# Attention with two feed-forward layers: words converted later, parked sums copied and stored by ScalarE

## The chip, the cores and the metric

One NeuronCore of one Trainium2 chip runs the whole kernel. The metric is the device time of one execution in microseconds (us), taken as the median of several runs. TensorE (PE) multiplies matrices and writes its results to PSUM banks, VectorE (DVE) and ScalarE (ACT) do elementwise work, GpSimd (POOL) does a little, and SyncE (SP) issues DMAs. Each engine takes its own instructions strictly in order and waits where a result of another engine is missing.

## The reference

Three layers follow each other. Attention: 4 batches, 8 heads, head size 64, 512 local tokens and 32 global ones. Global queries see all 544 keys; a local query sees the 32 global keys and the local keys at most 32 positions away. The result has 2176 rows of 512 numbers.

```python
s_ll = np.where(np.abs(pos[:, None] - pos[None, :]) <= 32, scale * q_l @ k_l.T, -1e9)
a_l = softmax(concat([scale * q_l @ k_g.T, s_ll]))     # local rows; global rows see k_all
x = a @ concat([v_g, v_l])                             # (2176, 512) over batches and heads
h = x @ w_in1;  x = (max(h, 0) ** 2) @ w_out1          # d_ff = 2048
h = x @ w_in2
P = a0 + a1*h + a2*h**2 + a3*h**3
Q = 1 + |b0|*|h| + |b1|*h**2
out = (P / (Q + 1e-6)) @ w_out2
```

The four weight matrices arrive as 64-bit floats; all else is 32-bit.

## The kernel before, in words

**Weights.** Each layer's hidden dimension is cut into 16 slices f of 128. A slice has two halves, a piece of `w_in` (half 0) and one of `w_out` (half 1). A half arrives as 64-bit words and has to be made into 32-bit floats by integer work; then it is split into a high and a low part, so that three fast matmuls give a 32-bit product. Here one half is called a *word item*. Its steps, with their engines: load into a tile `S` (SP, `w_load`, L125); `abs` (ACT, L142), which takes a fresh tile `T`; `elow` (POOL, L150); `clamp`, `shift`, `sign`, `add` (DVE, L145, L156, L160, L165); then `hi` and `lo`. For the first five slices `hi` is an ACT copy into the weight tile (L178) and `lo` a DVE subtraction (L185). For slices 5 to 10 of the first layer, `hi` is an SP store of the finished `T` to a scratch tensor in HBM (L170) and `lo` does nothing; the item is read back later.

**Ticks.** `cv_tick` is the clock of these steps. At each tick every item under way grows one tick older and does the steps whose age is listed in its table; every `per` ticks a new item is loaded. The item keeps the table that `cv["at"]` held when it was loaded. `OX` has `abs` at age 8, `clamp` at 9, `add` at 10, `hi` at 13, `lo` at 14. There are three `S` tiles and four `T` tiles.

**The attention stage.** 41 steps i = 0 to 40, five to a unit (half a batch's heads). Each step issues the scores of one group, softmax work of others, transposes (`T`, `tr`), the product with the values (`PV`) of group i, and four ticks at its end. Vectors of `v` are loaded into window tiles (`vw`, `big`) and then copied inside SBUF by four DMAs (L608 to L611).

**Fill jobs.** From step F0 = 11 on, TensorE also does part of the first feed-forward layer in each attention step: `f_h` (`H`, L511, 12 matmuls) for job i-11 and `f_y` (`Y`, L541, 12 matmuls) for the job before it. Jobs run over tokens in segments of 256 with slices 0 to 4. At the last job of a segment the two banks `Y` hold a sum that is *parked*: copied to two tiles `pk` (L551) and stored to the HBM tensor `park` (L552); the two segments that add to an earlier sum load it first (L518) and add on DVE (L548). The `pk` tiles come out of the same four as `T`. Sums without an addition are parked at steps 13, 15, 26, 31, 36 and after step 40, called parks 1 to 6; those with an addition at steps 18 and 21. In steps from 11 on, `tr`, `T`, `PV` and `H` have one PSUM bank each, so the next user of a bank waits until ACT or DVE has read it.

**DMA counters.** Every DMA raises one of eight completion counters, used in turn. A DMA waits for the one that used its counter before it. In the listings below `DMAHW5_49` is counter 5; `PE_49`, `DVE_49`, `Activation_49`, `Pool_49` are the counters of the engines.

**After the attention** the rest of both layers runs, 699 us, with TensorE the busy engine.

Of the kernel before, what the change touches and what calls it, by code (L numbers as in the profile page):

```python
# [23 lines left out]
def kernel(  # L24
# [36 lines left out]
    pe, ve, sc, gp, sy = nc.tensor, nc.vector, nc.scalar, nc.gpsimd, nc.sync  # L61
# [4 lines left out]
    def bank(tag):  # L66
        i = turns[tag].pop(0)
        turns[tag].append(i)
        return ps.tile([128, 512], F32, tag=f"b{i}", name=tag)
# [123 lines left out]
    todo, line, cv = [], [], dict(z=4, at=None, per=8, lo=ve)  # L193
# [22 lines left out]


    OX = dict(abs=8, elow=8, clamp=9, shift=9, sign=9, add=10, hi=13, lo=14)
    OE = dict(abs=4, elow=4, clamp=5, shift=5, sign=5, add=6, hi=9, lo=10)
    OL = dict(abs=2, low=3, clamp=3, shift=4, sign=4, add=5, hi=7, lo=9)  # L220
    OS = dict(hi=5, lo=8)
    ORD = ("hi", "add", "lo", "clamp", "shift", "sign", "low", "elow", "abs")
# [259 lines left out]
    def fill(i):  # L482
        return fp.tile([128, (10, 4, 2)[i] * NSUB], F32, tag=f"f{i}", name=f"f{i}")

    frows, fturn, fx, fh, fg, fy, fpk = [], dict(x=0, h=0), {}, {}, {}, [], []
# [16 lines left out]
    def f_park(a, i):  # L502
        return park[:, 2 * i:2 * i + 2, NSUB * a:NSUB * a + NSUB]

    def f_h(q):
        seg, a, f, _, last, add = fjobs[q]
        while (0, f, 1) not in done:
            cv_tick(LEFT[1])
        w, h = wt[0, f], bank("H")[:, 0:NSUB]
        for m, (k, s, t) in enumerate([(k, s, t) for k in range(NK) for s, t in ((0, 0), (1, 0), (0, 1))]):  # L510
            pe.matmul(h, w[:, s, 0, 128 * k:128 * k + 128], fx[seg, k][t], start=m == 0, stop=m == 3 * NK - 1)  # L511
        if last:
            for k in range(NK):
                fx.pop((seg, k))
            if add:
                for i in range(2):
                    t = cv3.tile([128, 512], U32, tag="T", name="pk").bitcast(F32)
                    sy.dma_start(t.rearrange("p (m t) -> p m t", m=2), f_park(a, i))  # L518
                    fpk.append(t)
        i = fturn["h"] = (fturn["h"] + 1) % 2  # L520
        hi, lo = [frow(1, 2 * i + z).bitcast(F32R) for z in range(2)]
        g = frow(2, i)
        sc.activation(g, h, AF.Relu)
        sc.activation(hi, g, AF.Square)
        fh[q], fg[q] = (hi, lo), (g, h)
# [6 lines left out]
    def f_y(q):  # L532
        _, a, f, first, last, add = fjobs[q]
        hi, lo = fh.pop(q)
        w = wt[0, f]
        if first:
            fy[:] = [bank("Y"), bank("Y")]
        ms = range(NK)
        for m, z in [(m, z) for m in ms for z in range(2)] + [(m, 2) for m in ms]:

            pe.matmul(fy[m // 2][:, NSUB * (m % 2):NSUB * (m % 2) + NSUB], w[:, z % 2, 1, 128 * m:128 * m + 128],  # L541
                      (hi, hi, lo)[z], start=first and z == 0 and m % 2 == 0, stop=last and z == 2,
                      skip_group_check=True)
        if last:
            for i in range(2):
                if add:
                    t = fpk.pop(0)
                    ve.tensor_tensor(out=t, in0=fy[i], in1=t, op=ALU.add)  # L548
                else:
                    t = cv3.tile([128, 512], U32, tag="T", name="pk").bitcast(F32)  # L550
                    (sc.copy if i else ve.tensor_copy)(t, fy[i])  # L551
                sy.dma_start(f_park(a, i), t.rearrange("p (m t) -> p m t", m=2))  # L552


    with ExitStack() as at:
# [14 lines left out]
        def load_qk(n, i):  # L570

            b, hq = divmod(n, 2)
            src, dst, nm = ((q_l, qraw, "qr"), (k_l, kraw, "kr"))[i]
            t = raw1 if n == 1 and not i else raw.tile([128, 4, 4, D], F32, tag=nm, name=nm, bufs=1 + i)
            x = src[b, 4 * hq:4 * hq + 4].rearrange("h (p c) d -> c p h d", c=4)
            for c in range(4):
                sy.dma_start(t[:, c], x[c])
            dst[n] = t
# [10 lines left out]
        def load_v(n, part):  # L589
            b, hq = divmod(n, 2)  # L590
            hs = slice(4 * hq, 4 * hq + 4)
            w = vw[n % 2]
            wf = w.rearrange("p w h d -> p w (h d)")
            A, Bw, C = wf[:, 0:5], wf[:, 5:10], wf[:, 10:14]
            vg = v_g[b, hs].rearrange("h g d -> g h d")
            vl = v_l[b, hs]
            if part == 0:
                for a in range(5):
                    sy.dma_start(w[0:96, a, :, 0:D], vl[:, 96 * a:96 * a + 96].rearrange("h p d -> p h d"))
                sy.dma_start(w[96:128, 9, :, 0:D], vl[:, 480:512].rearrange("h p d -> p h d"))  # L600
                for p, a in ((96, 0), (64, 5), (32, 10)):
                    sy.dma_start(w[p:p + 32, a, :, 0:D], vg)
                return
            if part == 2:
                for p, t, m in ((96, A, 4), (64, Bw, 4), (32, C, 3)):
                    gp.tensor_copy(t[p:p + 32, 1:], t[p:p + 32, 0:1].to_broadcast([32, m, 4 * (D + 1)]))
                return
            sy.dma_start(Bw[0:64], A[32:96])  # L608
            sy.dma_start(Bw[96:128, 0:4], A[0:32, 1:5])
            sy.dma_start(C[0:32], A[64:96, 0:4])  # L610
            sy.dma_start(C[64:128], A[0:64, 1:5])  # L611
# [13 lines left out]
        for i, pair in enumerate(some):  # L625
            for h in range(4):
                p, m = slice(32 * h, 32 * h + 32), pair[h % 2]
# [91 lines left out]
        F0 = 11  # L719
# [165 lines left out]
        for i in range(NS + 1):  # L885
            (n, g), pos, fq = groups[min(i, NS - 1)], i % 5, i - F0
            if i == F0 - 1:
                turns.update(T=[2], PV=[3], tr=[4])
                frows.extend(fill(z) for z in range(3))
            for c in (LD0 if n == 0 else LD)[pos] if i < NS else ():  # L890
                if c in "qk":
                    m = n + 2 + (c == "k" and pos == 4)
                    if m < 2 * B:
                        load_qk(m, "qk".index(c))
                elif n + 1 < 2 * B:
                    load_v(n + 1, "ABR".index(c))
            if i + 2 < NS:
                pend.pop(i + 2)()
            late = i + 2 < NS and groups[i + 2][1] == 4
            quo = list(st_r.pop(i - 1)) if i else []  # L900
            low = []
            if i + 3 < NS and not late:
                low, pend[i + 3] = do_S(i + 3)
            for op in itertools.chain(*itertools.zip_longest(quo, low)):
                if op:
                    op()
            for dn, z in PZ0[pos] if n == 0 else PZ[pos]:
                if i < NS and n + dn < 2 * B:
                    prep(n + dn, z)

            if 0 <= fq < len(fjobs):
                f_h(fq)
            if i + 1 < NS:
                do_T(i + 1)
            if 0 <= fq < len(fjobs):
                f_low(fq)
            if i >= 2:
                do_xT(i - 2)
            if i + 3 < NS and late:
                low, pend[i + 3] = do_S(i + 3)  # L920
                for op in low:
                    op()
            if 0 < fq <= len(fjobs):
                f_y(fq - 1)
            if i < NS:
                do_PV(i)
            if fq == -1:
                for k in range(NK):
                    f_split(0, k)
            elif 0 <= fq:  # L930
                for d, ks in ((1, range(1, NK)), (2, range(1))):
                    if fq + d < len(fjobs) and fjobs[fq + d][3]:
                        for k in ks:
                            f_split(fq + d, k)
            if i == 0:
                prep_g(0)
            if i == 1:
                sy.dma_start(coef[:, 0:4], a2.rearrange("(o a) -> o a", o=1).to_broadcast([128, 4]))
                sy.dma_start(coef[:, 4:6], b2.rearrange("(o a) -> o a", o=1).to_broadcast([128, 2]))
            if i == 10:  # L940
                sc.activation(coef[:, 6:8], coef[:, 4:6], AF.Abs)
            if i == F0 - 3:
                cv.update(z=0, per=4)
            if i == F0:
                cv["at"] = OE
            if i == F0 + 3:
                cv["per"] = 7
            for _ in range(4):
                cv_tick(LEFT[1])
        do_xT(NS - 1)  # L950
# [44 lines left out]
```

## Time and profile before

| what | value |
|---|---|
| median of 3 runs | 948.52 us (947.42 to 950.25) |
| the profiled execution | 951.82 us, span of its instructions 950.0 us |
| TensorE busy | 906.0 us, 95% of the span |
| VectorE busy | 731.0 us, 77% |
| ScalarE busy | 619.6 us, 65% |
| attention stage | ends at about 251 us of the span |

The page gives, for one execution, the busy time of each engine, a strip of 40 slices of the span, DMA queues, the chain of work that ended last, and the costliest groups of instructions. Other views list the instructions of one engine in order of time (with the idle time before each and what ended it), sum waits by who waited for whom, or give busy time and granted TensorE clock by stretch. TensorE's busy time is near the span, but not evenly: the strip shows where it was not.

### The profile page before, as it was taken

To read this page: it belongs to the slowest core of one execution; us is meant where nothing else is said; L and a number is where in the kernel's file an instruction comes from. 1 tells how busy PE (TensorE), PEld (TensorE's weight loads), DVE (VectorE), ACT (ScalarE), POOL (GpSimd) and SP (SyncE) were. 2 spreads that over 40 slices of the span, in tenths; PEclk is the share of its full clock that TensorE was granted. 3 is DMA by queue.
4 is the path that set the end of the run, shared out by engine and by line. 5 is a ranking of instruction groups with operands and counts; after the bars stand their busy time and mean duration, and the time that the engine had idled before them with its cause. 6 is when DMAs were issued, how large, how long until landed. Compare 5 with 4: busy or idle time off the path is not lost.

```text
span 950.0 us, 19472 instructions
## 1 busy us (share of the span) xinstructions
PE 906.0 (95%) x7440; PEld 824.9 (87%) x7440; DVE 731.0 (77%) x1743; ACT 619.6 (65%) x1331; POOL 56.0 (6%) x109
## 2 busy tenths in 40 slices
PE   7886898998999999999999999999999999999997
PEld 4665787887899999999999998989989989989875
DVE  3687886778468577576766469999989989989896
ACT  3675664565478555454544457787787787787886
POOL 5223122120000000000000000000000000000000
PEclk9898799999999999999999999999999999999999
DMA  9997687662265264455422340010010010010000
GB/s 191 181 197 153 143 234 197 169 158 91 79 172 152 78 185 143 140 186 164 161 89 78 133 177 0 1 34 1 1 34 1 1 34 1 1 34 1 19 16 22
DMA packets 106477, 91.55 MB, mean 96 GB/s; under 512 B 60304, under 2 KB 89488, under 8 KB 106384
## 3 DMA queue, kind: packets, MB, share of 16 engines
q1 hardware_dynamic: 106384, 90.31, 35.6%
q8 instruction: 58, 0.95, 0.4%
q14 instruction: 35, 0.29, 0.1%
HBM read 63.18 MB, written 20.19 MB: 88 GB/s over the span
## 4 chain that ended last, share of the span: by engine, by line
PE 76%; DVE 7%; DMA 6%; ACT 6%; issue 2%; SPq 1%; ACTq 0%; DVEq 0%
PE S L306 31%; PE y L386 18%; PE y L383 13%; PE H L511 3%; DMA S<-in_moe_w_out_dram 3%; PE Y L541 3%; DMA S<-in_moe_w_in_dram 2%; PE tr L707 1%; PE S L740 1%; PE PV L834 1%; PE PV L839 1%; DVE T L160 1%; PE T L794 1%; DVE T L165 1%; DMA vw<-vw 1%
## 5 line engine op out<-in xcount | busy, mean ns | idle before, releaser
L306 PE MATMUL S<-big,w 128*128 128x384 f32 (+1 forms) x1776 | 330.7, 327 | 2.0 <-ACT big L288 1.1
L306 PEld LDWEIGHTS S<-big,w 128*128 128x128 f32 x1776 | 298.2, 188 | 9.1 <-DVE ts L346 2.1
L386 PE MATMUL y<-w,big 128*128 128x512 f32 x816 | 209.1, 398 | 4.2 <-ACT big L364 2.9
L386 PEld LDWEIGHTS y<-w,big 128*128 128x128 f32 x816 | 149.4, 188 | 38.2 <-DVE big L365 7.9
L383 PE MATMUL y<-big,w 128*128 128x384 f32 (+1 forms) x912 | 161.0, 326 | 1.7 <-DVE big L332 0.9
L383 PEld LDWEIGHTS y<-big,w 128*128 128x128 f32 x912 | 150.8, 188 | 2.4 <-DVE big L332 1.2
L342 ACT ACTIVATE big<-S 128x384 f32<-128x384 f32 (+1 forms) x96 | 45.6, 475 | 75.9 <-PE S L306 72.6
L321 ACT ACTIVATE big<-S 128x384 f32<-128x384 f32 (+1 forms) x76 | 35.6, 468 | 85.2 <-PE S L306 83.6
L329 DVE TENSOR_TENSOR big<-big 128x384 f32<-128x384 f32 (+1 forms) x60 | 31.3, 522 | 74.1 <-ACT big L325 73.9
L345 DVE TENSOR_TENSOR ts<-ts,S 128x384 f32<-128x384 f32 (+1 forms) x96 | 50.8, 529 | 24.8 <-ACT ts L343 24.5
L306 PE MATMUL S<-xm,w 128*128 128x384 f32 (+1 forms) x288 | 67.8, 327 | 0.0
L344 ACT ACTIVATE tq<-big,coef 128x384 f32<-128x384 f32 (+1 forms) x96 | 66.1, 689 | 0.0
L142 ACT ACTIVATE T<-S 128x512 f32<-128x512 f32 x64 | 42.9, 670 | 34.2 <-DMA S<-in_moe_w_in_dram 13.4
L343 ACT ACTIVATE ts<-S,coef 128x384 f32<-128x384 f32 (+1 forms) x96 | 62.5, 651 | 0.0
L346 DVE SCALAR_TENSOR_TENSOR ts<-ts,coef,S 128x384 f32<-128x384 f32 (+1 forms) x96 | 56.9, 592 | 3.4
L325 ACT ACTIVATE big<-big 128x384 fp32r<-128x384 f32 (+1 forms) x76 | 38.2, 503 | 30.2 <-PE y L383 29.7
L306 PEld LDWEIGHTS S<-xm,w 128*128 128x128 f32 x288 | 52.2, 188 | 2.9
L358 DVE SCALAR_TENSOR_TENSOR ts<-tq,ts 128x384 f32<-128x384 f32 (+1 forms) x96 | 51.4, 536 | 3.3
L541 PE MATMUL Y<-f,w 128*128 128x256 f32 x360 | 52.1, 295 | 1.2 <-ACT pk L551 1.2
L511 PE MATMUL H<-f,w 128*128 128x256 f32 x360 | 52.3, 296 | 0.0
L365 DVE TENSOR_TENSOR big<-ts,big 128x384 fp32r<-128x384 f32 (+1 forms) x96 | 50.7, 528 | 0.2 <-ACT big L364 0.2
L347 DVE TENSOR_TENSOR tq<-tq,big 128x384 f32<-128x384 f32 (+1 forms) x96 | 50.7, 529 | 0.0
(132 smaller groups left out, 1314.9 us busy)
## 6 DMA issues: line engine op xcount, KB each, us to landing
S<-in_moe_w_out_dram SPq DMA_DIRECT2D x32, 512.0 KB, 4.3
S<-in_moe_w_in_dram SPq DMA_DIRECT2D x32, 256.0 KB, 5.6
S<-in_moe_w_in_dram SPq DMA_DIRECT2D x16, 512.0 KB, 4.6
scr<-T SPq DMA_DIRECT2D x24, 256.0 KB, 2.5
T<-scr SPq DMA_DIRECT2D x24, 256.0 KB, 2.8
both<-stg SPq DMA_DIRECT2D x10, 512.0 KB, 3.4
w<-both SPq DMA_DIRECT2D x10, 512.0 KB, 4.3
out_dram<-xT SPq DMA_DIRECT2D x17, 256.0 KB, 2.6
```

Of the source, the lines that this page charges most:

```text
L306: pe.matmul(h, wk[k][s], x[k][t], start=m == 0, stop=m == 3 * NK - 1)
L343: sc.activation(s, h, AF.Identity, scale=coef[:, 3:4], bias=coef[:, 2:3])
L344: sc.activation(q, av, AF.Identity, scale=coef[:, 7:8], bias=coef[:, 6:7])
L345: ve.tensor_tensor(out=s, in0=s, in1=h, op=ALU.mult)
L346: ve.scalar_tensor_tensor(out=s, in0=s, scalar=coef[:, 1:2], in1=h, op0=ALU.add, op1=ALU.mult)
L347: ve.tensor_tensor(out=q, in0=q, in1=av, op=ALU.mult)
L358: ve.scalar_tensor_tensor(out=s, in0=q, scalar=2.0, in1=s, op0=ALU.subtract, op1=ALU.mult, reverse0=True)
L365: ve.tensor_tensor(out=lo, in0=s, in1=hi.bitcast(F32), op=ALU.subtract)
L383: pe.matmul(y[m][:, 0:n], a, x, start=st and z == 0, stop=sp and z == 2)
L386: pe.matmul(y[m], a, x, start=st and z == 0, stop=sp and z == 2)
L511: pe.matmul(h, w[:, s, 0, 128 * k:128 * k + 128], fx[seg, k][t], start=m == 0, stop=m == 3 * NK - 1)
L541: pe.matmul(fy[m // 2][:, NSUB * (m % 2):NSUB * (m % 2) + NSUB], w[:, z % 2, 1, 128 * m:128 * m + 128], (hi, hi, lo)[z], start=first and z ...
```

## The change

Three edits. The table `OE`, for word items loaded later in the attention stage, gets the ages of `OX` for `abs` to `add` and keeps `T` until age 17 before it is stored. The switch from `OX` to `OE` moves from step 11 to step 14. Both halves of a parked sum without an addition are copied by ACT, and each is stored by a DMA that ACT issues; sums with an addition are still stored by SP.

```diff
-    OE = dict(abs=4, elow=4, clamp=5, shift=5, sign=5, add=6, hi=9, lo=10)
+    OE = dict(abs=8, elow=8, clamp=9, shift=9, sign=9, add=10, hi=17, lo=18)
...
-                    (sc.copy if i else ve.tensor_copy)(t, fy[i])
-                sy.dma_start(f_park(a, i), t.rearrange("p (m t) -> p m t", m=2))
+                    sc.copy(t, fy[i])
+                (sy if add else sc).dma_start(f_park(a, i), t.rearrange("p (m t) -> p m t", m=2))
...
-            if i == F0:
-                cv["at"] = OE
             if i == F0 + 3:
-                cv["per"] = 7
+                cv.update(at=OE, per=7)
```

Counting items 1 to 10 (slices 0 to 4) and 11 to 22 (slices 5 to 10): before, items 1 to 7 used `OX` and 8 to 22 `OE`; now 1 to 10 use `OX`. Item 10 ends at tick 70, and the job of step 17 needs it, so two ticks run there before the job's matmuls; later loads stand two ticks earlier in the program.

ACT at step 13, from the transposed scores to the next step's exponentials. `pk` is a half of park 1, `T<-S` the `abs` of an item. Before:

```order
L812 COPY big_234<-tr 128x128
L551 COPY pk<-Y 128x512 [waits DMAHW6_49,DVE_49,PE_49]
L498 CAST f_1248<-xT 128x256
L178 CAST w_1540<-T 128x512
L142 ACTIVATE T<-S 128x512 [waits DMAHW1_49,DMAHW7_49,DMAHW0_49,Activation_49]
```

After:

```order
L812 COPY big_234<-tr 128x128
L551 COPY pk<-Y 128x512 [waits PE_49]
L552 DMA park<-pk 128x2x256 [waits DMAHW5_49,Activation_49]
L551 COPY pk<-Y 128x512 [waits DVE_49,PE_49]
L552 DMA park<-pk 128x2x256 [waits DMAHW0_49,Activation_49]
L498 CAST f_1248<-xT 128x256
L178 CAST w_1540<-T 128x512
L142 ACTIVATE T<-S 128x512 [waits DMAHW5_49,DMAHW3_49]
```

Before, ACT's copy waited for counter 6, the store of park 1's other half, because both halves were given the same tile; now neither copy waits for a DMA, and the `abs` behind them (item 8) waits for counter 5, which the first store on ACT raises.

SP at the same place, the in-SBUF copies of a `v` tile and what follows. Before:

```order
L608 DMA vw_112<-vw_112 64x1300 [waits DMAHW2_49]
L609 DMA vw_112<-vw_112 32x1040 [waits DMAHW3_49]
L610 DMA vw_112<-vw_112 32x1040 [waits DMAHW4_49]
L611 DMA vw_112<-vw_112 64x1040 [waits DMAHW5_49]
L552 DMA park<-pk 128x2x256 [waits DMAHW6_49,DVE_49]
L552 DMA park<-pk 128x2x256 [waits DMAHW7_49,Activation_49]
L125 DMA S<-in_moe_w_out_dram 128x1024 [waits DMAHW0_49,DVE_49]
```

After:

```order
L609 DMA vw_112<-vw_112 32x1040 [waits DMAHW5_49]
L610 DMA vw_112<-vw_112 32x1040 [waits DMAHW6_49]
L611 DMA vw_112<-vw_112 64x1040 [waits DMAHW7_49]
L125 DMA S<-in_moe_w_out_dram 128x1024 [waits DMAHW0_49,DVE_49,Activation_49]
```

The two stores left SP, and L609 and the next load now wait for counters 5 and 0, which are those of ACT's two stores.

SP from step 24 to step 27, around park 3; `S` loads are those of items 16 and 17. Before:

```order
L125 DMA S<-in_moe_w_out_dram 128x1024
L170 DMA scr<-T 128x512
L599 DMA big_111<-in_v_l_dram 96x4x64 x5
L600 DMA big_111<-in_v_l_dram 32x4x64
L602 DMA big_111<-in_v_g_dram 32x4x64 x3
L552 DMA park<-pk 128x2x256 x2
L125 DMA S<-in_moe_w_in_dram 64x4x256 x2
```

After:

```order
L170 DMA scr<-T 128x512
L125 DMA S<-in_moe_w_in_dram 64x4x256 x2
L599 DMA big_111<-in_v_l_dram 96x4x64 x5
L600 DMA big_111<-in_v_l_dram 32x4x64
L602 DMA big_111<-in_v_g_dram 32x4x64 x3
L170 DMA scr<-T 128x512
```

The load of item 17 stood behind the two park stores; now it stands ahead of the nine `v` loads, one step earlier, and its `abs` keeps its step.

## Rows read from the trace of the kernel before

**Rows 1.** The page: busy time by engine, and the strip of the granted clock

```profile
PE 906.0 (95%) x7440; PEld 824.9 (87%) x7440; DVE 731.0 (77%) x1743; ACT 619.6 (65%) x1331; POOL 56.0 (6%) x109
...
PEclk9898799999999999999999999999999999999999
```

**Rows 2.** Busy time by stretch: steps 13 to 17, steps 18 to 40, the rest

```profile
core 0: us, PE busy (x) PEld busy (x) DVE busy (x) ACT busy (x) POOL busy (x), PEclk, DMA share, GB/s
...
77.50:121.80 44.30, 33.89 (x494) 28.92 (x493) 33.42 (x107) 23.38 (x64) 7.71 (x10) 0.81 0.65 160
121.80:251.00 129.20, 121.18 (x1983) 108.25 (x1982) 93.53 (x326) 69.95 (x189) 22.58 (x27) 0.97 0.58 149
251.00:950.00 699.00, 686.52 (x3805) 641.48 (x3803) 554.93 (x1099) 480.41 (x953) 0.00 (x0) 1.00 0.23 73
```

**Rows 3.** TensorE's waits, 77 to 251 us: total us, times, longest

```profile
PE PV L839 <- DVE xs L845: 8.0, 2, 5.3
PE PV L834 <- DVE xs L845: 4.1, 3, 3.1
PE tr L860 <- ACT kt L715: 3.1, 2, 1.9
PE tr L810 <- ACT kt L715: 1.9, 1, 1.9
PE Y L541 <- ACT pk L551: 1.2, 1, 1.2
```

**Rows 4.** TensorE in order of time: start, duration, [idle before <- what ended it]

```profile
77.51 1.68 PE L511 MATMUL H<-f,w 128*128 128x256 f32 x12
...
121.84 1.67 PE L511 MATMUL H<-f,w 128*128 128x256 f32 x12
...
161.01 0.95 PE L839 MATMUL PV<-big,pt 96*32 96x65 f32 x32 [2.66 <-DVE xs L845]
...
253.55 6.71 PE L306 MATMUL S<-big,w 128*128 128x384 f32 x36 [1.09 <-ACT big L288]
```

**Rows 5.** ScalarE in order of time

```profile
89.70 0.59 ACT L551 COPY pk<-Y 128x512 f32<-128x512 f32 x1 [7.17 <-DMA park<-pk]
...
155.73 0.69 ACT L142 ACTIVATE T<-S 128x512 f32<-128x512 f32 x1 [3.44 <-issue]
...
176.81 0.38 ACT L523 ACTIVATE f<-H 128x256 f32<-128x256 f32 x1 [0.73 <-PE H L511]
...
182.03 0.67 ACT L142 ACTIVATE T<-S 128x512 f32<-128x512 f32 x1 [3.42 <-issue]
...
209.86 0.67 ACT L142 ACTIVATE T<-S 128x512 f32<-128x512 f32 x1 [3.36 <-DMA S<-in_moe_w_out_dram]
```

**Rows 6.** VectorE in order of time

```profile
90.62 0.42 DVE L499 TENSOR_TENSOR f<-xT,f 128x256 fp32r<-128x256 f32 x1 [6.52 <-ACT f L498]
...
120.97 0.16 DVE L848 TENSOR_SCALAR sm<-PV 128x1 f32<-128x1 f32 x1 [1.05 <-PE PV L839]
```

**Rows 7.** The copies of parked sums: duration in ns, least, median, most

```profile
L551 DVE COPY pk<-Y x6: 683/690/692, 83.4 to 252.3; 128x512 f32<-128x512 f32 x6
L551 ACT COPY pk<-Y x6: 587/587/589, 89.7 to 252.5; 128x512 f32<-128x512 f32 x6
```

**Rows 8.** The stores of parked sums, L552: issue time in ns, and time to landing

```profile
L552 SPq DMA_DIRECT2D park<-pk x16: 360/399/1117, 84.2 to 253.5; - x16
...
DMA to landing us min/median/max: 2.1/2.5/5.4
```

**Rows 9.** SP's issues in order of time: start, duration

```profile
63.12 1.89 SPq L125 DMA_DIRECT2D S<-in_moe_w_out_dram  x1
...
175.13 1.60 SPq L552 DMA_DIRECT2D park<-pk  x2
```

**Rows 10.** Two stretches behind waits, columns as in rows 2

```profile
160.00:166.00 6.00, 4.99 (x69) 4.33 (x70) 3.10 (x12) 1.79 (x4) 1.16 (x2) 0.72 0.47 152
215.00:220.00 5.00, 3.68 (x45) 2.32 (x46) 3.66 (x19) 1.28 (x4) 1.53 (x2) 0.66 0.55 174
```

## The prediction, made before the changed kernel was run

> **What bounds the kernel now.** I read the strip of the page first. TensorE is granted nearly its full clock everywhere but in three of the first five slices [rows 1], so the loss lies in the attention stage. The windows say where: steps 13 to 17 take 44.3 us with TensorE busy for 33.9 at a mean granted clock of 0.81, steps 18 to 40 take 129.2 with 121.2 busy, and behind 251 us TensorE is busy 686.5 of 699 [rows 2]. The change touches only the first 253 us; what it saves there moves the rest forward whole, since the rest starts from the end of the attention and is bound by TensorE.
>
> TensorE's waits from 77 to 251 us add up to 18.3 us in nine places [rows 3]. Followed back, they have one pattern. ACT, whose instructions stand in a row, waits for a DMA; DVE waits for ACT; TensorE waits for DVE to empty the one `PV` bank. The largest is park 1: ACT sat idle 7.17 us before its copy of the second half, until the store of the first had landed [rows 5], DVE sat idle 6.52 us behind it [rows 6], TensorE 1.2 and 5.3 us [rows 3], and then it ran at a low clock. Three more start at an `abs` (L142) whose word had not landed: 3.44, 3.42 and 3.36 us on ACT [rows 5]. Their word was late because SP, also in order, stood before the stores of parked sums and of words until DVE had finished them.
>
> **The change part by part.** The sum is made against the profiled execution, 951.82 us, of which 950.0 are the span; it lies 3.3 us above the median of 948.52, within what the runs scatter.
>
> *Steps 13 to 17.* At park 1 fewer words are under way (item 8 now takes its `T` only at step 13's end), so both halves get tiles of their own, and the 7.17 us go. Next late is DVE: in these steps one word item per step is converted. Over the stretch DVE was busy 33.42 of 44.3 us [rows 2], the stretch being that between the `H` of step 13 and that of step 18 [rows 4]. The item steps in it are the same before and after (five items converted, five `lo`), shifted by one step; what leaves DVE is two copies of 0.69 [rows 7]. That makes 33.42 - 1.38 = 32.0 us, so at most 12.3 us can go. Some DVE waits are TensorE's own (1.05 us at 120.97 [rows 6]); I keep 1.3 for these: 11.0. New waits come in: the `abs` of items 8 and 10 now stand behind the ACT stores of parks 1 and 2 and wait until the first half of each has landed. Between that store's issue and the `abs` ACT has a copy, a second issue and one or two casts, some 2 us; landing took 2.5 us in the median, 5.4 for the slowest [rows 8]. So 0.5 to 3.4 us each on ACT, partly covered because DVE still has one item's steps to do. I take 0.5 each, near the median: -1.0. Worth of this part: **10 us**, between 4 and 12.3. The lower end has two landings of 5.4, about 1.5 us each uncovered, and 3 us for L609: SP's copies of the `v` tile now wait for ACT's first store, and the `PV` of step 15 needs them.
>
> *Steps 18 to 40.* The `abs` comes 8 ticks, two steps, behind its load instead of 4. A step is about 5.6 us (129.2 by 23), so each word gets that much more, which is above the longest wait of 3.44. Words are stored 7 ticks behind their `add`, so SP no longer stands before them. The TensorE waits that end with these three `abs` are the smaller of the two L839 waits (8.0 - 5.3 = 2.7, at 161.01 [rows 4]), the longest of L834 (3.1) and the smaller tr wait (3.1 - 1.9 = 1.2) [rows 3]: 7.0 us. Behind the first and second the clock fell: 0.72 over 6 us with 4.99 busy, 0.66 over 5 us with 3.68 busy [rows 10]; a share of (1 - clock) of the busy time is lost, 1.4 + 1.25 = 2.7. Together 9.7. What is late next is again DVE, in the steps that convert a word: the two other L834 waits (4.1 - 3.1 = 1.0 for both [rows 3]) are of this kind and stay, and I let three more of 0.5 to 0.6 come: -1.7. Worth: **8 us**, between 5 and 9.7.
>
> *ACT copies and issues, parks at steps 26, 31 and 36.* Each adds to ACT one copy of 0.59 [rows 7] and two DMA issues. The trace has no issue on ACT; the nearest rows are SP's own issues of the same stores, 0.36 at least, 0.40 in the median, 1.12 at most [rows 8]. I take the median, since the transfer is the same: 0.59 + 0.80 = 1.39 us a park. Behind the copy ACT has the exponentials and a `tr` copy and then waits for `H`, 0.73 us in the first of the three places [rows 5]; that is the cover, and the other two I take alike. About 0.66 stays uncovered a park, and only some of it meets a TensorE wait, the `tr` bank being due within a us. **-1 us**, between 0 and 3 x (0.59 + 2.24 - 0.73) = -6.3. DVE loses 0.69 at each; it is not counted. SP loses its twelve issues; its time is not on the path.
>
> *Park 6, after step 40.* Here nothing covers. ACT's second copy came at the same time as DVE's, then ACT prepares the next stage's first input while TensorE waits, 1.09 us already [rows 4]. Now ACT does both copies and both issues first: 0.59 + 0.80 = **-1.4 us**, between -0.6 and -2.8.
>
> *At no cost:* the four DMAs of the two sums with an addition stay on SP. The two extra ticks in step 17 only split item 10's low part, which `Y` needs a step later. Loads come two ticks earlier; the three `S` tiles suffice, as an item frees its own 10 ticks after its load and is followed in it 12 or 21 ticks after.
>
> Sum: 10 + 8 - 1 - 1.4 = 15.6 us. 951.8 - 15.6 = 936.2 for an execution like the profiled one; from the median, 948.5 - 15.6 = **932.9**, rounded to 933.0.
>
> **The rivals.** *1. ACT pays more for the DMAs than SP does, or the stores land late: 941 us.* Issue at SP's longest, 1.12 us: parks 3 to 5 cost 6.3 and park 6 costs 2.8, which is 6.7 more than in the sum, and parks 1 and 2 lose about 1.5 more. 933 + 8 = 941. For it: SP's issues were at times long, 1.89 us for one load [rows 9]. Against: the median is 0.40. The Trainium skill, Perfetto Trace Analysis, "DMA Instruction — HWDGE (DVE, Sync)", says that one descriptor generator serves both issuing sequencers and that an issue waits for its lock; by that rule an ACT store beside an SP load would take as long as SP's issue does. No row of this trace can show it, since only SP issues.
>
> *2. Slower: ACT is held at each issue as long as SP was held by its long loads, 952 to 954 us.* At 1.89 us for each of twelve issues [rows 9], ACT gets 12 x 1.49 = 17.9 us more than in the sum, all of it at places where DVE or TensorE follow within a us. That is 2.3 more than the 15.6 gained, and the clock, which took 2.7 us behind two waits above, takes 1 to 3 more: 952 to 954. It decides from 0.4 + 15.6 / 12 = 1.7 us an issue on. Against it: SP stood at 1.60 for a pair of park stores [rows 9].
>
> *3. It does not do what it should: 946 to 951 us.* ACT's waits go, but DVE, busy three quarters of steps 13 to 17, takes their place: if TensorE must wait for DVE in each step and the clock stays as low as 0.81 [rows 2], TensorE's 33.9 busy us are not shortened and the steps keep some 40 us. Then 4 + 5 remain of the two large parts at their low ends, and rival 1's prices for ACT, 6.3 + 2.8, take them away: 948.5 - 9 + 9.1 = 948.6, and 946 to 951 around it.
>
> *4. More: 925 us.* All bounds at their good end: 12.3 + 9.7 - 0 - 0.6 = 21.4, and DVE's relief at parks 3 to 5 gives back 2. 948.5 - 23.4 = 925.
>
> **How the numbers follow.** The forecast (928 to 938) has 0.55, rival 1 (938 to 945) 0.2, rival 4 (below 928) 0.11, rival 3 0.09, rival 2 0.05. About 0.3%, 2.8 us, is what a measurement of this kernel can tell from no change: faster is below 945.7, slower above 951.4. Faster: 0.55 + 0.2 + 0.11 = 0.86; within: 0.09; slower 0.05. The range that leaves two in ten outside goes from 924 (half of rival 4's tail) to 944.
>
> **What would show it.** Steps 13 to 17, from `H` to `H`, should take about 34 us, with DVE idle for under 2 and the clock near 0.95. No `abs` from step 17 on should wait over 1 us for a load. The ACT issues of L552 should take 0.4 us; at park 1 ACT should wait 0.5 to 3 us in the `abs` of item 8. TensorE's waits up to 251 us should fall from 18 to about 5. The first FFN matmul should wait 2.5 us instead of 1.09. The stage behind should take 699 us as before. The prediction is wrong if ACT's issues are long, if DVE is full in steps 13 to 17 and TensorE no faster, or if SP's copies behind ACT's first store come too late for step 15.

## The result and the profile after

| | before | after |
|---|---|---|
| median, us | 947.97 (945.88 to 950.25) | 936.57 (935.12 to 938.0) |
| ratio | | 0.9879, 95% interval 0.985 to 0.9909 |
| profiled execution | 951.82 | 937.45, span 935.7 |

The change makes the kernel 11.4 us (1.2%) faster, between 8.6 and 14.2 by the interval. The forecast was 933.0, in a range from 924 to 944.

The page of the kernel after: busy time, and the strip of the granted clock, where the second and third dip of [rows 1] are gone.

```profile
PE 900.9 (96%) x7440; PEld 821.3 (88%) x7440; DVE 729.5 (78%) x1737; ACT 623.8 (67%) x1337; POOL 55.5 (6%) x109
...
PEclk9899999999999999999999999999999999999999
```

Busy time by stretch of the kernel after, columns as in [rows 2]: steps 13 to 17, steps 18 to 40 (up to the first matmul of the last `H`, step 40's), from there to the first L383 matmul (here called the seam), the rest.

```profile
75.93:112.70 36.77, 30.09 (x495) 26.12 (x494) 32.30 (x99) 23.68 (x63) 8.60 (x10) 0.95 0.80 200
112.70:233.97 121.27, 116.98 (x1951) 104.25 (x1949) 91.59 (x322) 70.84 (x190) 21.07 (x27) 0.99 0.64 162
233.97:249.85 15.88, 13.41 (x86) 13.10 (x81) 4.78 (x11) 8.69 (x18) 0.00 (x0) 0.89 0.21 70
249.85:935.70 685.85, 675.73 (x3757) 631.61 (x3756) 551.03 (x1092) 473.83 (x940) 0.00 (x0) 1.00 0.23 72
```

The same stretches of the profile before were 44.33, 125.19, 13.07 and 689.90 us; the second and third:

```profile
121.84:247.03 125.19, 117.17 (x1950) 104.24 (x1948) 91.88 (x321) 68.67 (x186) 22.58 (x27) 0.97 0.59 154
247.03:260.10 13.07, 11.98 (x88) 11.43 (x81) 5.52 (x12) 7.76 (x17) 0.00 (x0) 1.00 0.36 122
```

So the profile gains 7.6 us in steps 13 to 17 and 3.9 in steps 18 to 40, and loses 2.8 in the seam. Another 1.6 lie ahead of step 13, where the programs differ little; the `H` of step 13 starts between 75.4 and 78.2 us in all but one of the kernels below, so this may be scatter. The 4.05 us of the last stretch are probably scatter too: that stretch, the same instructions in all kernels below, took 684.4 to 689.0 us in their twelve profiles, and the 689.90 of before lie 0.9 above the highest of these.

TensorE's waits from 76 to 250 us in the kernel after (total us, times, longest). They add up to 13.2 us. The 18.3 of [rows 3] leave out the wait of 1.09 us at the first L306 [rows 4]; without the 2.5 us of the same place it is 10.7 against 18.3. The third to the fifth line are new ones.

```profile
PE PV L839 <- DVE xs L845: 3.7, 2, 2.2
PE S L306 <- ACT big L288: 2.5, 1, 2.5
PE S L740 <- DVE nmx L746: 2.3, 2, 1.2
PE tr L810 <- ACT big L710: 1.6, 1, 1.6
PE H L511 <- DVE w L185: 1.2, 1, 1.2
```

ACT in the kernel after around parks 1 and 2, in order of time. The 7.17 us of [rows 5] are gone: both copies follow each other. But the `abs` of items 8 and 10 stand for 3.79 and 2.10 us until a park store has landed.

```profile
79.49 0.58 ACT L551 COPY pk<-Y 128x512 f32<-128x512 f32 x1 [0.71 <-PE Y L541]
80.11 0.39 ACTq L552 DMA_DIRECT2D park<-pk  x1
80.59 0.58 ACT L551 COPY pk<-Y 128x512 f32<-128x512 f32 x1 [0.51 <-ACT pk L551]
81.20 0.37 ACTq L552 DMA_DIRECT2D park<-pk  x1
...
86.33 0.66 ACT L142 ACTIVATE T<-S 128x512 f32<-128x512 f32 x1 [3.79 <-DMA park<-pk]
...
99.49 0.69 ACT L142 ACTIVATE T<-S 128x512 f32<-128x512 f32 x1 [2.10 <-DMA park<-pk]
```

Step 32 in the kernel after, ACT, DVE and TensorE in order of time: park 4's two copies and two issues, then an `abs`; DVE stands 3.06 us at its clamp (L145) until that `abs` is done, not for the DMA that the row names, and everything behind the clamp on DVE, the emptying of `PV` among it, comes late.

```profile
188.50 0.59 ACT L551 COPY pk<-Y 128x512 f32<-128x512 f32 x1 [0.27 <-PE Y L541]
189.11 0.37 ACTq L552 DMA_DIRECT2D park<-pk  x1
...
190.19 0.37 ACTq L552 DMA_DIRECT2D park<-pk  x1
...
190.66 0.68 ACT L142 ACTIVATE T<-S 128x512 f32<-128x512 f32 x1 [0.50 <-DMA S<-in_moe_w_in_dram]
...
191.37 0.43 DVE L145 TENSOR_SCALAR T<-T 128x512 f32<-128x512 f32 x1 [3.06 <-DMA park<-pk]
...
195.04 0.66 PE L834 MATMUL PV<-big,pt 128*32 128x65 f32 x32 [0.62 <-DVE xs L845]
```

### The profile page after: what moved, and what is told of

Its sections match the earlier page's. It is cut to its first block, busy times and chain, and to the rows that moved or that the text cites. A ratio compares the mean times of both kernels' runs of the same rounds, so it can differ in the third digit from the quotient of the medians.

```text
span 935.7 us, 19475 instructions
## 1 busy us (share of the span) xinstructions
PE 900.9 (96%) x7440; PEld 821.3 (88%) x7440; DVE 729.5 (78%) x1737; ACT 623.8 (67%) x1337; POOL 55.5 (6%) x109
## 4 chain that ended last, share of the span: by engine, by line
PE 82%; DVE 6%; ACT 5%; DMA 4%; issue 1%; SPq 0%; ACTq 0%; DVEq 0%
PE S L306 33%; PE y L386 18%; PE y L383 15%; PE H L511 4%; PE Y L541 4%; DMA S<-in_moe_w_in_dram 2%; PE S L740 2%; PE tr L707 1%; PE PV L834 1%; PE T L794 1%; PE PV L839 1%; DMA vw<-vw 1%; DMA park<-pk 1%; ACT pk L551 1%; DMA pk<-park 1%
## 5 line engine op out<-in xcount | busy, mean ns | idle before, releaser
L306 PE MATMUL S<-big,w 128*128 128x384 f32 (+1 forms) x1776 | 330.8, 327 | 3.5 <-ACT big L288 2.5
L306 PEld LDWEIGHTS S<-big,w 128*128 128x128 f32 x1776 | 298.6, 189 | 10.3 <-ACT big L288 2.7
L383 PE MATMUL y<-big,w 128*128 128x384 f32 (+1 forms) x912 | 159.7, 325 | 0.3 <-DVE xT L393 0.3
L383 PEld LDWEIGHTS y<-big,w 128*128 128x128 f32 x912 | 149.8, 188 | 0.6 <-DVE xT L393 0.6
L306 PE MATMUL S<-xm,w 128*128 128x384 f32 (+1 forms) x288 | 67.8, 328 | 0.0
L306 PEld LDWEIGHTS S<-xm,w 128*128 128x128 f32 x288 | 52.1, 188 | 2.9
L511 PEld LDWEIGHTS H<-f,w 128*128 128x128 f32 x360 | 47.2, 199 | 3.9 <-DVE w L185 1.4
```

The lines of the kernel that those rows point to most:

```text
L306: pe.matmul(h, wk[k][s], x[k][t], start=m == 0, stop=m == 3 * NK - 1)
L383: pe.matmul(y[m][:, 0:n], a, x, start=st and z == 0, stop=sp and z == 2)
```

## The experiments

The stretches are read from the timeline of each kernel's profile; ratios are to the kernel before on the same chip, with 95% intervals.

| kernel | median, us | ratio | steps 13-17 | 18-40 | seam |
|---|---|---|---|---|---|
| before | 947.97 | 1 | 44.33 | 125.19 | 13.07 |
| the whole change | 936.57 | 0.9879 (0.985-0.9909) | 36.77 | 121.27 | 15.88 |
| words_only | 939.8 | 0.9915 (0.9885-0.9946) | 43.73 | 117.63 | 13.17 |
| parks_only | 939.24 | 0.9919 (0.9887-0.9951) | 42.08 | 116.23 | 15.76 |
| switch_only | 946.24 | 0.9982 (0.9952-1.0012) | 41.81 | 126.12 | 13.06 |
| copies_split | 943.87 | 0.9951 (0.9928-0.9974) | 41.34 | 121.63 | 16.05 |
| parks_1_2 | 932.78 | 0.9855 (0.9829-0.988) | 36.59 | 116.61 | 13.17 |
| parks_switch | 940.58 | 0.9928 (0.9902-0.9955) | 35.78 | 123.86 | 15.87 |
| own_tiles | 935.53 | 0.9889 (0.9863-0.9914) | 33.97 | 119.01 | 15.76 |
| stores_on_sp | 936.77 | 0.9905 (0.987-0.9941) | 39.29 | 117.35 | 13.31 |
| own_1_2 | 932.24 | 0.9848 (0.9817-0.9879) | 37.13 | 117.28 | 13.17 |
| own_1_2_lo12 | 945.18 | 0.9997 (0.9975-1.002) | 45.06 | 118.57 | 13.08 |
| own_1_2_no606 | 930.81 | 0.9804 (0.9777-0.9831) | 34.25 | 115.36 | 13.06 |
| whole_no606 | 936.99 | 0.9882 (0.985-0.9913) | 37.09 | 120.59 | 15.83 |

### The parts alone

The edit of words_only is that of the table and the switch; parks_only has the two lines of the parks; switch_only has the last hunk without the table. copies_split is the whole change with one line put back:

```diff
-                    sc.copy(t, fy[i])
+                    (sc.copy if i else ve.tensor_copy)(t, fy[i])
```

> Only the table OE and the switch at step 14 are changed; parked sums are copied by DVE and ACT and stored by SP, as before. Theory A (the words carry the whole gain, and ACT's copies and issues take some of it back): steps 13 to 18 take about 37 us as with the whole change, step 32 falls from 8.7 to about 6.5 us since ACT reaches the abs behind park 4 about 1.5 us earlier, and the way from the last H to the first L383 is 13.1 us again instead of 15.9. 936.6 - 2.8 - 2 = 932 us, ratio to the kernel before 0.981 to 0.985. Theory B (the parks on ACT's queue are needed too, since SP standing before park stores holds the loads): an abs waits 2 to 3.5 us for its load at the steps behind parks 3 to 5, and steps 13 to 18 take over 39 us: 941 to 945 us.

> Only the copies and stores of parked sums without an addition are changed (both copies on ACT, both stores issued by ACT); the words keep the old table and switch. Theory A: both halves of park 1 still get the same tile, so ACT's second copy waits for the landing of the first store, 2.5 to 6 us instead of 7.2; that saves 1 to 4 us, the late words between steps 18 and 40 stay, and the seam behind step 40 costs 2.8: 946 to 950 us, no change that can be told. Theory B (SP freed of the park stores is worth something by itself): the abs waits of 3.4 us in steps 24 to 33 go, and the time is 941 to 944 us.

> Only the switch from OX to OE is moved from step 11 to step 14; OE keeps its old ages and the parks are as before. Theory A (park 1 is slow because both halves get one tile; later words free a second): steps 13 to 18 take 37 to 39 us instead of 44.3, ACT's wait of 7.2 us at park 1 is gone, steps 18 to 40 stay at 125 us with their three late words: 940 to 942 us. Theory B (the gain in steps 13 to 18 comes from SP being freed or DVE's two copies): steps 13 to 18 take 42 us or more, 946 to 949 us.

> The whole change, but the first half of a parked sum is copied by DVE again; ACT still copies the second and issues both stores. Theory A (ACT is the late one at parks 4, 5 and behind step 40): the abs behind park 4 comes 0.6 us or more earlier, step 32 falls below 8 us, and from the last H to the first L383 it takes 15 us or less instead of 15.9: 934 to 935.5 us. Theory B (DVE is the late one, so its 0.69 us a copy count): steps 13 to 18 take 37.5 to 38.5 us instead of 36.8 and the whole 937 to 939 us.

In steps 13 to 17 no part does alone what they do together: 43.7, 42.1 and 41.8 us against 36.8. My theory A was wrong there for the words and for the switch; both theories of copies_split missed (41.3 us and 943.9), and theory A of parks_only missed by the time, 939.2 instead of 946 to 950. Of theory B of words_only only the steps' over 39 us came true. words_only shows one reason; a second, POOL beside DVE in step 13, comes further below. Its first fence is ACT: park 1's tile conflict is gone, as forecast (1.87 us instead of 7.17), but the next three `abs` wait for DVE's L185, which frees the `T` tile they take. The second is DVE and SP: the copy on DVE comes at 85.48, behind DVE's word steps, and the stores leave SP 8.0 us after the `H` of step 13 (78.23); with the whole change the first left ACT 4.2 us after it (80.11 and 75.93).

```profile
82.95 0.59 ACT L551 COPY pk<-Y 128x512 f32<-128x512 f32 x1 [1.87 <-DVE sm L848]
...
89.81 0.68 ACT L142 ACTIVATE T<-S 128x512 f32<-128x512 f32 x1 [5.45 <-DVE w L185]
97.74 0.66 ACT L142 ACTIVATE T<-S 128x512 f32<-128x512 f32 x1 [3.45 <-DVE w L185]
```

```profile
85.48 0.68 DVE L551 COPY pk<-Y 128x512 f32<-128x512 f32 x1
...
86.19 0.98 SPq L552 DMA_DIRECT2D park<-pk  x2
```

parks_only keeps the conflict: ACT's second copy waits for the landing of the first store, as theory A had it. copies_split has the copy on DVE late again, and now ACT stands before the issue of its store (the 5.55 us end with DVE's copy, 83.71 to 84.39, not with the matmul named). ACT's timeline at park 1, first in parks_only, then in copies_split:

```profile
87.69 0.59 ACT L551 COPY pk<-Y 128x512 f32<-128x512 f32 x1 [6.32 <-DMA park<-pk]
```

```profile
84.43 0.38 ACTq L552 DMA_DIRECT2D park<-pk  x1
84.85 0.59 ACT L551 COPY pk<-Y 128x512 f32<-128x512 f32 x1 [5.55 <-PE S L765]
```

In steps 18 to 40 it is the other way about: words_only alone brings 7.6 us and parks_only 9.0, both together only 3.9. That the two don't add up is no surprise, since both work on the same late words; but together they bring less than either. Their steps differ in three places: step 32 takes 8.70 us with both, 6.85 and 5.72 with one; step 33 6.81 against 5.37; step 37 6.58 against 5.12 and 5.02. Only with both does an `abs` stand right behind park 4 and park 5 on an ACT that has two copies and two issues to do first. With one copy and two issues (copies_split) the three steps still take 8.81, 6.91 and 6.69.

### Which parks, and which ages

parks_1_2 keeps ACT's copies and stores for parks 1 and 2 alone; parks_switch is the whole change with the old `OE`.

```diff
-                    sc.copy(t, fy[i])
-                (sy if add else sc).dma_start(f_park(a, i), ...)
+                    (sc.copy if i or a < 2 else ve.tensor_copy)(t, fy[i])
+                (sc if a < 2 and not add else sy).dma_start(f_park(a, i), ...)
```

> The whole change for the words; parks 1 and 2 are copied and stored by ACT, parks 3 to 6 are copied by DVE and ACT and stored by SP as before. Theory A (ACT's two copies and two issues ahead of an abs make steps 32 and 37 late and the first FFN matmuls late; in steps 13 to 17 they help, since there DVE is the late engine): steps 13 to 18 take 36.8 us as with the whole change, steps 18 to 40 take 117.6 as with the words alone (32 falls from 8.7 to 6.9, 37 from 6.6 to 5.1), from the last H to the first L383 13.1 instead of 15.9; together 6.4 us less: 930 us, ratio to the kernel before about 0.981. Theory B (what steps 32 and 37 lose comes from the words' later loads and stores, not from ACT): only the 2.8 us behind step 40 come back, 934 us.

> The whole change but for the table OE, which keeps its old ages (abs 4 ticks behind the load, store at 9); the switch is at step 14 and the parks are on ACT. Theory A (with SP freed of the park stores the loads come early enough, and a word whose abs is not late needs no more ticks): steps 13 to 18 take 36.8 us, steps 18 to 40 take 116.2 as with the parks alone: 936.6 - 5 = 931.5 us. Theory B (two steps between load and abs are needed): an abs of steps 18 to 40 waits 2 to 3.5 us for its load again, these steps take 121 us or more: 936 to 941 us.

parks_1_2 came out as theory A had it: 36.6, 116.6 and 13.2 us. By its profile it is 7.6 us shorter than the whole change up to the first L383. By the medians it is 3.8 us faster, but these come from different chips; by the ratios, 0.9855 and 0.9879, it is 2.3 us, and their intervals overlap. At step 32 DVE's clamp waits 0.73 us there instead of 3.06. With the old ages three `abs` of steps 20 to 24 wait 2.92, 2.67 and 1.99 us for their loads again, and steps 18 to 40 lose 7.3 us against parks_1_2, all of it in steps 20 to 27: theory B. So with the switch at step 14 the two steps between load and `abs` are needed. They are not needed as such: parks_only has the old ages too, with the switch at step 11, and took 116.2 us there, with no `abs` waiting over 2.1. Why the later switch makes the old ages late stays open. The steps of parks_1_2 in busy time, then ACT and DVE at step 32, from the timeline:

```profile
112.48:229.09 116.61, 115.05 (x1950) 102.82 (x1948) 94.98 (x325) 69.02 (x187) 21.44 (x26) 1.00 0.65 163
```

```profile
189.10 0.67 ACT L142 ACTIVATE T<-S 128x512 f32<-128x512 f32 x1
```

```profile
189.81 0.43 DVE L145 TENSOR_SCALAR T<-T 128x512 f32<-128x512 f32 x1 [0.73 <-ACT T L142]
```

### Which queue

stores_on_sp is the whole change with `sy.dma_start` for all parks.

> The whole change, but SP issues the stores of all parks; ACT does both copies. Theory A (at park 1 the queue counts: behind SP's copies of the v tile the store starts some 5 us later than on ACT, and the abs that takes the tile waits for it): the abs of item 8 waits 5 us or more, steps 13 to 18 take 40 to 42 us, while the steps from 18 on gain about 1 us each at parks 4 and 5 from the two issues that ACT is spared: 938 to 941 us. Theory B (only the copies count): steps 13 to 18 take 36.8 us and the time is 934 to 936 us.

Neither theory holds as it stands. Steps 13 to 17 take 39.3 us, nearer to theory A, but the `abs` do not wait for a store: three wait for DVE's L185, 4.80 us at the longest. Steps 18 to 40 gain 3.9, the seam 2.6, and the median is that of the whole change within the scatter (933.5 to 943.2), as theory B had it for the time. At step 32 DVE's clamp waits 1.99 us: 3.06 with two copies and two issues on ACT, 1.99 with two copies, 0.73 with one. So about 1.1 of the 2.3 us that the clamp waits longer are the issues, and 1.3 the copy.

The seam shows a second price. The 36 first L306 matmuls in stores_on_sp, where ACT has two copies but no issue ahead of them (timeline), and the 3 us from their start (busy time, columns as in [rows 2]):

```profile
240.06 6.71 PE L306 MATMUL S<-big,w 128*128 128x384 f32 x36 [1.34 <-ACT big L288]
```

```profile
240.06:243.06 3.00, 3.00 (x16) 2.65 (x17) 1.94 (x4) 1.60 (x4) 0.00 (x0) 1.00 0.98 308
```

The same in the kernel after, where the issues are on ACT too, with ACT's first instruction behind them:

```profile
241.86 8.15 PE L306 MATMUL S<-big,w 128*128 128x384 f32 x36 [2.47 <-ACT big L288]
```

```profile
241.30 1.75 ACT L288 CAST big<-xT 128x384 fp32r<-128x384 f32 x4 [0.44 <-ACT pk L551]
```

```profile
241.86:244.86 3.00, 3.00 (x10) 2.88 (x11) 1.94 (x4) 1.19 (x3) 0.00 (x0) 0.54 0.59 188
```

Behind the wait of 1.34 us the clock stays at 1.00; behind 2.47 it is 0.54 for the next 3 us, mostly the lower of the two levels (1.2 of 2.4 GHz), and the 36 matmuls take 8.15 us instead of 6.71. It is the same in all fourteen profiles: the wait is 1.09 us with DVE's copy and SP's stores and 1.34 with two copies on ACT, the clock 1.00; with ACT's issues it is 2.46 to 2.63 and the clock 0.50 to 0.57. So the second copy costs TensorE 0.25 us here and the two issues 1.13.

### The abs behind the park stores

own_tiles copies parks 1 to 5 to unused columns of two big tiles; own_1_2 does so for parks 1 and 2 and treats parks 3 to 6 as before.

```diff
-                    t = cv3.tile([128, 512], U32, tag="T", name="pk").bitcast(F32)
+                    t = (big1, big2)[i][:, 512:1024] if a < 5 else cv3.tile(...).bitcast(F32)
```

> The whole change, but parks 1 to 5 are copied to 512 unused columns of two big tiles instead of two of the four T tiles, so that no abs waits for a park store. Theory A (the waits of 3.8 and 2.1 us of the abs of items 8 and 10 are on the path): steps 13 to 18 take 33 to 34.5 us instead of 36.8, and the time is 932 to 934.5 us. Theory B (DVE, busy 32.3 us there, is late anyway): the two waits of ACT go, steps 13 to 18 take 35.8 us or more: 935.5 to 937 us.

> Two findings put together: parks 1 and 2 are copied by ACT to unused columns of two big tiles and stored from ACT's queue; parks 3 to 6 are copied by DVE and ACT to T tiles and stored by SP as before; the words as in the whole change. Theory A (the parts add up, since they lie in different steps): steps 13 to 18 take 34.0 us as with own tiles, steps 18 to 40 take 116.6 and the way to the first L383 13.2 as with parks 1 and 2 on ACT; together 2.6 us less than that kernel's 932.8: 930 us. Theory B (what steps 13 to 18 gain is given back in the steps behind, as it was partly with own tiles, 935.5 us instead of the 932 that its steps promised): 931.5 to 933 us.

In the profile of own_tiles the `abs` of item 8 comes 1.3 us after the end of the second copy instead of 5.2, and steps 13 to 17 take 33.97 us at clock 1.00 with DVE busy for 31.5: theory A, and the forecast's 34. ACT's timeline, and the busy time of the steps:

```profile
83.06 0.67 ACT L142 ACTIVATE T<-S 128x512 f32<-128x512 f32 x1
```

```profile
76.61:110.58 33.97, 28.55 (x496) 24.64 (x494) 31.51 (x100) 23.73 (x63) 7.02 (x9) 1.00 0.84 197
```

The median, 935.53, does not show it: 1 us less than the whole change, with overlapping intervals and the higher ratio. In steps 18 to 40 it takes 2.3 us less, and step 33 falls from 6.81 to 5.37, so that part of the price goes by the tiles and not by ACT's copies and issues. And own_1_2, whose `abs` waits are gone as well, took 37.1 us there instead of theory A's 34.0, and 932.24 in the median, the same as parks_1_2 within the scatter. In its profile DVE's word steps of step 13 run beside POOL's copies (L606), in order of time:

```profile
78.18 3.82 POOL L606 COPY vw<-vw 32x1040 f32<-32x1040 f32 x3
78.43 1.42 DVE L160 SCALAR_TENSOR_TENSOR T<-S,T 128x512 uint32<-128x512 uint32 x1
79.98 1.32 DVE L165 CUSTOM_DVE_ANT_0 T<-S,T 128x1024 uint16<-128x1024 uint16 x1
81.23 1.31 DVE L185 TENSOR_TENSOR w<-T,w 128x512 fp32r<-128x512 f32 x1
```

They take 1.3 to 1.4 us instead of 0.69. Two kernels without these copies from the third unit on test that:

```diff
-                for p, t, m in ((96, A, 4), (64, Bw, 4), (32, C, 3)):
+                for p, t, m in ((96, A, 4), (64, Bw, 4), (32, C, 3)) if n < 2 else ():
```

> As the kernel with own tiles for parks 1 and 2, but the copies on POOL that spread the global rows of v over the window tiles (L606) are left out from the third unit on, so part of the values is stale. Theory A (in the profile of that kernel steps 13 to 18 took 37.1 us instead of 34.0 because DVE's word steps ran beside L606 and took 1.3 to 1.4 us instead of 0.69; these excesses add up to 3.2): DVE's L160, L165 and L185 at step 13 take 0.69 each and steps 13 to 18 take 33.5 to 34.5 us. Theory B (DVE is slowed by the DMAs of the v tile or of the parks): they keep 1.0 us or more, and the steps take 36 us or more.

> The whole change, with the same copies on POOL (L606) left out from the third unit on. Theory A (with the whole change steps 13 to 18 take 36.8 us because the abs of items 8 and 10 wait for the landing of park stores, and L606 met none of DVE's long steps there): the two waits stay at 2 to 4 us, and steps 13 to 18 take 36 to 37 us, 2 to 3 more than the kernel with own tiles and without L606. Theory B (the waits on park stores are covered, and POOL beside DVE is the whole difference): they take within 1 us of that kernel.

In DVE's timeline of own_1_2_no606 the same three rows are

```profile
77.72 0.69 DVE L160 SCALAR_TENSOR_TENSOR T<-S,T 128x512 uint32<-128x512 uint32 x1
78.55 0.69 DVE L165 CUSTOM_DVE_ANT_0 T<-S,T 128x1024 uint16<-128x1024 uint16 x1
79.16 0.69 DVE L185 TENSOR_TENSOR w<-T,w 128x512 fp32r<-128x512 f32 x1
```

and steps 13 to 17 take 34.25 us. With the whole change the `abs` waits stay (4.06 and 2.37 us) and the steps take 37.09. Both theories A hold, on one profile each: the waits on park stores are worth 2.8 us of these steps, and POOL beside DVE can take the same again.

Whether the two meet is decided before the parks. The sources of own_1_2, parks_1_2 and the whole change differ only from park 1's copies on, yet L606 starts 0.5, 3.4 and 3.4 us after the `H` of step 13. So it can differ from execution to execution; that own tiles are not seen in the medians for this reason is likely, but not shown. POOL's copies stand beside step 13's word steps in words_only, switch_only, copies_split, parks_switch and stores_on_sp too: TensorE waits 1.5 to 2.3 us there for step 13's `PV` bank, 0.4 in the whole change, parks_1_2 and own_tiles, and the step takes 1.1 to 3.0 us longer than the 5.84 of the whole change. So that much of what they lose in steps 13 to 17 can be POOL and not the part that was left out. In words_only POOL, DVE and TensorE:

```profile
79.49 4.07 POOL L606 COPY vw<-vw 32x1040 f32<-32x1040 f32 x3
```

```profile
81.33 1.53 DVE L185 TENSOR_TENSOR w<-T,w 128x512 fp32r<-128x512 f32 x1
```

```profile
84.23 0.93 PE L834 MATMUL PV<-big,pt 128*32 128x65 f32 x32 [2.23 <-DVE xs L845]
```

The remaining 3.9 of the 7.0 us between words_only and the whole change stand in the steps behind, with the three `abs` waits above.

### A repair that failed

TensorE waits 1.2 us at step 17 for DVE's L185, in the kernel after, behind the two extra ticks. own_1_2_lo12 ends each item two ticks earlier.

```diff
-    OX = dict(abs=8, elow=8, clamp=9, shift=9, sign=9, add=10, hi=13, lo=14)
+    OX = dict(abs=8, elow=8, clamp=9, shift=9, sign=9, add=10, hi=11, lo=12)
```

> As the kernel with own tiles for parks 1 and 2, and OX makes the high part at age 11 and the low part at 12 instead of 13 and 14, so that item 10 is done by the end of step 16 and no two ticks run ahead of the matmuls of step 17. Theory A (TensorE's wait of 2.0 us in step 17 is due to the two extra ticks, which put a word's four DVE steps ahead of that job): the wait falls below 0.5, step 17 takes 6 to 6.5 us instead of 8.3: 928 to 929 us. Theory B (the low part is late because DVE is full, whatever the ticks): the wait moves to step 16 or stays, and the time is that of the kernel it is made from within 1 us.

It lost 13 us, which neither theory had; whether the two ticks cause the wait of step 17 stays open. ACT's copy of the high part now stands one tick behind DVE's `add`, and ACT waits for it with all of its queue behind, seven times between 62 and 121 us, by 0.9 to 6.85 us. The longest, in ACT's timeline:

```profile
85.94 0.62 ACT L178 CAST w<-T 128x512 fp32r<-128x512 f32 x1 [6.85 <-DVE T L165]
```

## Why the prediction was right or wrong

**Direction and range** were right, and so was the mechanism of the two large parts; the price of ACT's queue was too low, and the time with it, by 3.6 us. At the first L383 the profile had gained 10.25 us of the 15.6 forecast. That the profiled execution, 937.45, is so near the 936.2 forecast for it is luck: 4.05 of its 14.4 us lie in the last stretch, where nothing was forecast. Of the signs, TensorE's waits were to fall to about 5 us and fell to 10.7, DVE was to be idle for under 2 us in steps 13 to 17 and was for 4.5, and one `abs` behind step 17, in step 20, still waited 1.41 us.

**Steps 13 to 17**, forecast 10 us, measured 7.6. That ACT's 7.17 us would go, that DVE would be next late and that it would be busy for 32.0 us were right (32.30). The step that failed is the price of the two `abs` behind ACT's stores: I took 0.5 us each from the median landing, the trace shows 3.79 and 2.10, the first store needing 6.1 us to land. The 2.5 was the median over all parks, but the landing goes by the place: the 5.4 of [rows 8] is park 1's own first store, which took 3.8 to 6.5 us in every kernel here whose row tells it, while those after step 40 took 2.1 to 2.9. From issue to landing, the four stores of parks 1 and 2 in the kernel after:

```profile
DMA to landing us min/median/max: 3.4/4.8/6.1
```

The Trainium skill, Perfetto Trace Analysis, "DMA Instruction — HWDGE (DVE, Sync)", says that the confirmation of a write can take surprisingly long, above all to HBM; the 2.1 to 6.1 us of these stores agree, though no row parts the confirmation from the transfer. Without the two waits the forecast's 34 us came out twice, 33.97 and 34.25, and a third time 37.13 with POOL beside DVE. TensorE waits 1.2 us in step 17, behind the two extra ticks that were put at no cost. SP's L609 did stand 6.1 us for ACT's first store, as feared, but the `PV` of step 15 followed without a wait.

**Steps 18 to 40** were forecast at 8 us for the words. parks_1_2, where ACT has only its old copy at parks 3 to 5, gained 8.6, and words_only 7.6: this term was right. The new ages are not the only way to it: parks_only gained 9.0 without them.

**ACT at parks 3 to 5**, forecast -1 us, measured -4.7 (121.27 against 116.61). It stayed inside its bounds, 0 to -6.3, but the value was mis-sized by its cover. I read from the trace of before that exponentials and a wait for `H` follow the copy. In the new order an `abs` follows it at parks 4 and 5, with DVE's clamp behind it. At park 3 nothing was lost: steps 26 and 27 took 11.6 us, as in parks_1_2.

**Park 6**, forecast -1.4, measured -2.8. The sum of the wait was right (2.5 forecast, 2.47 measured), by luck: the copy was put at 0.59 and cost 0.25, the two issues at 0.80 and cost 1.13. The clock behind it, 1.44 us, was not in the sum, though a fall of the clock behind two other waits stood in [rows 10].

**The issue's own time** was right: 0.37 us on ACT, 0.40 taken from SP. What it takes out of ACT's order is more: between two copies, or a copy and a cast, it makes 0.54 to 0.60 us in the seam (ACT's copies start 1.08 us apart with an issue between them, 0.48 in stores_on_sp). Rivals 1 and 2 fell in their main term all the same; what rival 1 said of late landings came true, and by the kernels without the two waits it is the miss of steps 13 to 17. ACT's issues in the kernel after (duration in ns, then the landing of all L552 stores in us):

```profile
L552 ACTq DMA_DIRECT2D park<-pk x12: 366/366/386, 80.1 to 240.9; - x12
...
DMA to landing us min/median/max: 2.1/2.5/6.1
```

**The two theories that the change mixes**: its two halves help each other in steps 13 to 17 and hurt each other in steps 18 to 40. That the sum of the parts is not the whole was not in the prediction. In steps 13 to 17 part of that help can be POOL's, as said above.

**Left open**: why the pool hands the `abs` a tile that DVE frees when SP stores, and one that a park store frees when ACT does; and the medians of own_1_2_no606 and whole_no606 differ by 6.2 us, their profiles by 11.6 at the first L383; the profiled execution of the first, 926.7 us, was the shortest of its four.

## What to carry to other kernels

Moving a copy and its store to a less busy engine pays where the old engine is the late one (parks 1 and 2) and costs where the next thing on the new engine's queue is awaited by a third (parks 4 to 6), so decide it place by place: parks_1_2 has the gain of the one without the cost of the other. Price a landing by the rows of the same place, not by the median of all. Read the cover of a moved step from the order of the changed kernel, not from the rows of the old one. A wait of TensorE that grows is to be priced with the slow matmuls that can follow it.

## What the runs showed of the hardware

- DVE beside POOL: the same three DVE instructions took 1.42, 1.32 and 1.31 us beside POOL's copies and 0.69 without them. The Trainium skill, SBUF — State Buffer, "Who interferes with whom", says that a DVE instruction with two SBUF inputs contends with a GpSimd instruction that reads SBUF; the rows agree. POOL's three copies themselves took 3.82 us instead of the 3.12 that they took in own_tiles behind those steps.
- An issue on ACT beside one on SP: in own_1_2 ACT's issue at 82.87 lies within SP's at 82.74, and took 0.40 us, SP's 0.59, as its neighbours did. No wait of one for the other beyond 0.03 us can be seen there; rival 1 had allowed for one as long as SP's issue. The two rows, from the timelines of ACT and SP:

```profile
82.87 0.40 ACTq L552 DMA_DIRECT2D park<-big  x1
```

```profile
82.74 0.59 SPq L608 DMA_DIRECT2D vw<-vw  x1
```
